# The first batch's step-1 sums in SBUF, turned by PE, in a fused FFT-mix and SoLU kernel

## The chip, the cores and the metric

The kernel runs on one core of one Trainium2 chip. The metric is the device time of one launch in microseconds, from the start of the program to its end. Engines are called as the profile calls them: PE (TensorE matmul), PEld (its weight load), DVE (VectorE), ACT (ScalarE), POOL (GpSimd), SP (SyncE, which here issues nearly all DMAs).

## What is computed

Eight batches of 3136 tokens with 256 channels. Along the tokens a real Fourier transform is taken, the spectrum is mixed by a complex 256x256 weight, biased and soft-thresholded, and transformed back; each token of the result then goes through a SoLU layer with 1024 hidden channels and a layer norm.

```python
X = rfft(x, axis=1); Xr, Xi = X.real, X.imag
Yr = Xr @ w_r - Xi @ w_i + b_r
Yi = Xr @ w_i + Xi @ w_r + b_i
Y  = soft(Yr, 0.01) + 1j * soft(Yi, 0.01)          # soft: sign(v) * max(|v| - 0.01, 0)
y  = irfft(Y, n=3136, axis=1)                       # 8 x 3136 x 256
h  = y @ w_in                                       # 25088 x 1024
s  = h * softmax(h)
out = (layernorm(s) * g_ln) @ w_out                 # 25088 x 256
```

## The kernel before

**The transform in two steps.** 3136 is 98 x 32. Step 1 sums over 98 (token index n1) for each of 32 n2; step 2 sums over the 32. The inverse has the same two steps. Step 1 of batches 0 and 1 is `fwd1_plain`: eight tiles of 98 x 1024 (n1 on the partitions, four n2 x 256 channels along them), in each two matmuls with the 98x98 matrix `fa_s` as the stationary operand and 512 columns of x moving, all in f32. ACT copies the sums out of PSUM, and SP stores them to a DRAM tile `s1f`. Step 2 needs pairs of (frequency, n2) on the partitions, so `load_bin` loads them back from `s1f` in that order: six groups `g` of four blocks of 128 x 256, and a last half block in `fwd2_last`. Each block is scaled by `scales[b]["s1"]`, a power of two found from the peak of x, and split into a high and a low f16 half (`bin`), the high half by ACT, the low by DVE. `fwd2` multiplies them with `fb_s`, `mix` with the complex weights, `threshold` follows, `inv1` is the first inverse step, whose sums are stored to DRAM (`s2f`, for batch 0), and `inv2` loads them back into `zt` tiles, makes the second inverse step with `iaf_s` and fills `ring_hi` and `ring_lo`, the tokens for SoLU. `moe_head`, `moe_turn` and `moe_tail` are SoLU for 128 tokens each.

**Weights.** The mix weights `w_hi`, `w_lo` have five parts; three are made early, and `later_mix_weights` makes the other two from sums and differences. Their raw matrices lie in two tiles named `zt` (lines 1169 to 1172), of a pool with two buffers of that name: the first loads of `inv2` reuse these buffers. `moe_w_in` loads and splits w_in into `win_hi`, `win_lo`, `win_low`; `moe_w_out` and `finish_w_out` do so with w_out. Their scales are found from a peak over all partitions, by a reduction on DVE, a transpose on PE (`ident,wpeak` in the profile), a reduction of the row (`wtop`), and a product with ones that spreads it.

**What sets the order.** All operations of the program are recorded first, and a planner (`Plan`, lines 286 to 495) then puts them in a fixed order on each engine; all instructions are issued on line 396. It is a list scheduler: an operation has a key (`nc.key`, a smaller key is more urgent), a length estimated in `weigh`, and the operations that it needs; on the engine that can start first, the one with the smallest key is taken among those that can start within 105 ns of the first. An operation gives no urgency to those that it needs. Tiles of one name get their buffers in turn, and a buffer is free again when the last operation that reads it is done. `nc.hold(op)` makes an operation wait for another one that it doesn't need. Each engine then works its own list strictly in order, so that a waiting instruction holds up all behind it, and a waiting DMA on SP all later DMAs of SP. The keys of the parts are in `KEYS` (lines 42 to 53): the first part of the program has keys from -200, `later_mix_weights` has 254.87, and the first `inv2` has -122.76.

**Lines touched.** `fwd1_plain` 709, `load_bin` 747, `fwd2_last` 775, `x_scale` 618, `w3` 1169, `win_*` 1239, `wout` 1241, `ring_lo` 1028, `moe_w_out` 1277, and the main part from 1344.

## Time and profile before

| | us |
|---|---|
| median of 3 runs (lowest, highest) | 1536.11 (1534.29, 1539.84) |
| span of the profiled execution | 1532.7 |
| PE busy in it | 1506.8 (98%) |
| DVE busy | 1223.0 (80%) |
| ACT busy | 1182.7 (77%) |
| POOL busy | 1139.1 (74%) |
| median minus span | 3.4 |

The profile is one execution on the chip, seen by the hardware profiler. An engine's busy time is the time in which it has an instruction in work; an idle time is put down to what released the next instruction. The granted clock is what PE was given in a stretch, 1.00 for 2.4 GHz and 0.50 for 1.2 GHz. An f32 matmul leaves two records in the trace, a transpose or an f16 matmul one. Line L396 stands on all rows, since all instructions are issued there; the tile names tell them apart, with buffer numbers left out (`w_hi` for w0_hi and w1_hi).

### The profile page before, as it was taken

The numbers are of one execution on the slowest core, as the hardware profiler recorded it, in microseconds if no ns is written. First come the engines' busy times: TensorE is split into PE (matmuls) and PEld (weight loads), VectorE is DVE, ScalarE is ACT, GpSimd is POOL, SyncE is SP. The second block draws the span as 40 slices with busy tenths as digits, with TensorE's granted clock in tenths as the row PEclk, the third lists the DMA queues.
The fourth block names the chain that finished last, engine by engine and source line by source line (L and its number), as shares of the span: only waits on it lengthen the run. The fifth ranks groups of instructions, "written<-read, shape, count | busy, mean of one in ns | idle before, by whom it ended". The sixth has DMA issues, their size and how long they took to land.

```text
span 1532.7 us, 40928 instructions
## 1 busy us (share of the span) xinstructions
PE 1506.8 (98%) x15375; PEld 1064.5 (69%) x15375; DVE 1223.0 (80%) x2496; ACT 1182.7 (77%) x2140; POOL 1139.1 (74%) x1652
## 2 busy tenths in 40 slices
PE   6989999999999999999999999999999999999998
PEld 3446777668766777677776777677776777776666
DVE  5888788888997988978788878978788778766664
ACT  5777878887797778877887778887788777777775
POOL 0656988777886887778876787758878688876776
PEclk8989999999999999999999999999999999999999
DMA  7777965999699987999689995899877976687666
GB/s 255 216 252 179 203 135 108 219 220 234 154 205 241 232 169 182 214 232 221 116 187 214 237 211 128 193 244 223 162 165 169 219 152 128 134 160 156 141 123 121
DMA packets 531580, 285.61 MB, mean 186 GB/s; under 512 B 426501, under 2 KB 504689, under 8 KB 531381
## 3 DMA queue, kind: packets, MB, share of 16 engines
q1 hardware_dynamic: 530932, 281.39, 83.0%
q8 instruction: 120, 1.97, 0.5%
q10 hardware_dynamic: 448, 1.61, 0.3%
q14 instruction: 80, 0.65, 0.1%
HBM read 103.07 MB, written 77.07 MB: 118 GB/s over the span
## 4 chain that ended last, share of the span: by engine, by line
PE 90%; DMA 3%; ACT 3%; POOL 2%; DVE 1%; issue 1%; SPq 0%; ACTq 0%; DVEq 0%; POOLq 0%
PE banks L396 90%; DMA xt<-in_x_dram 1%; DMA zt<-s2f 0%; DMA u<-in_x_dram 0%; POOL y L396 0%; DMA xt<-s1f 0%; POOL ll L396 0%; DMA zt<-in_w_r_dram 0%; ACT Xh L396 0%; DVE yt L396 0%; POOL r L396 0%; DMA zt<-s 0%; ACT zout L396 0%; DVE Xl L396 0%; SPq L396 0%
## 5 line engine op out<-in xcount | busy, mean ns | idle before, releaser
L396 POOL TENSOR_TENSOR ll<-u,lh 128x1024 f16<-128x1024 f32 x196 | 425.4, 2171 | 110.7 <-ACT lh L396 105.5
L396 PE MATMUL banks<-wout,th 128*128 128x256 f16 x3136 | 374.5, 273 | 0.2 <-DVE zout L396 0.2
L396 PEld LDWEIGHTS <-th 128*128 128x128 f16 x3136 | 304.5, 98 | 61.0 <-issue 1.9
L396 DVE SCALAR_TENSOR_TENSOR u<-banks,sm,u 128x1024 f32<-128x1024 f32 x196 | 251.1, 1281 | 105.0 <-ACT u L396 80.4
L396 DVE TENSOR_REDUCE sm<-banks 128x1 f32<-128x1024 f32 x196 | 239.2, 1220 | 79.8 <-PE banks L396 78.9
L396 PE MATMUL banks<-win_hi,ring_hi 128*128 128x512 f16 x768 | 292.0, 380 | 0.0
L396 PE MATMUL banks<-win_lo,ring_hi 128*128 128x512 f16 x768 | 291.8, 380 | 0.0
L396 PE MATMUL banks<-win_low,ring_lo 128*128 128x512 f16 x768 | 291.7, 380 | 0.0
L396 ACT CAST lh<-u 128x1024 f16<-128x1024 f32 x196 | 205.4, 1048 | 111.5 <-POOL a L396 57.2
L396 ACT ACTIVATE u<-banks,sm,hsb 128x1024 f32<-128x1024 f32 x192 | 231.2, 1204 | 61.3 <-DVE sm L396 51.6
L396 PEld LDWEIGHTS <-ring_hi 128*128 128x128 f16 x1536 | 148.7, 98 | 141.8 <-issue 2.3
L396 ACT ACTIVATE junk<-u,sm 128x1024 bf16<-128x1024 f32 x196 | 226.0, 1153 | 3.2 <-DVE u L396 3.1
L396 PE MATMUL banks<-wout,tl 128*128 128x256 f16 x1568 | 203.4, 273 | 0.0
L396 POOL TENSOR_TENSOR y<-yt,yc 128x512 f32<-128x512 f32 (+1 forms) x104 | 142.1, 1370 | 48.1 <-DVE yc L396 33.3
L396 PEld LDWEIGHTS <-tl 128*128 128x128 f16 x1568 | 151.8, 98 | 23.9 <-issue 1.0
L396 PE MATMUL banks<-w_hi,Xh 128*128 128x256 f16 (+1 forms) x584 | 165.4, 283 | 2.2 <-ACT Xh L396 1.8
L396 PE MATMUL banks<-w_hi,Xl 128*128 128x256 f16 (+1 forms) x584 | 165.0, 283 | 1.5 <-POOL Xl L396 0.9
L396 PE MATMUL banks<-w_lo,Xh 128*128 128x256 f16 (+1 forms) x584 | 165.2, 283 | 0.0
L396 POOL TENSOR_SCALAR a<-a,hsb 128x1 f32<-128x1 f32 x384 | 128.3, 334 | 14.7
L396 PEld LDWEIGHTS <-ring_lo 128*128 128x128 f16 x768 | 75.2, 98 | 91.1 <-issue 0.6
L396 PEld LDWEIGHTS <-Xh 128*128 128x128 f16 x1168 | 112.9, 98 | 31.7 <-issue 5.2
L396 POOL TENSOR_TENSOR yl<-y,yh 128x512 f16<-128x512 f32 x96 | 116.9, 1220 | 16.6 <-ACT yh L396 15.8
(177 smaller groups left out, 2512.6 us busy)
## 6 DMA issues: line engine op xcount, KB each, us to landing
xt<-in_x_dram SPq DMA_DIRECT2D x104, 392.0 KB
zt<-s SPq DMA_DIRECT2D x56, 392.0 KB
s<-zout SPq DMA_DIRECT2D x42, 512.0 KB
s<-av SPq DMA_DIRECT2D x48, 392.0 KB
bin<-s SPq DMA_DIRECT2D x36, 512.0 KB
out_dram<-o SPq DMA_DIRECT2D x128, 96.0 KB
out_dram<-o SPq DMA_DIRECT2D x136, 64.0 KB
out_dram<-o SPq DMA_DIRECT2D x128, 32.0 KB
```

The lines of the kernel that those rows point to most:

```text
L396: getattr(engine, name)(*args, **kw)
```

## The change

For batch 0 `fwd1_first` takes the place of `fwd1_plain`: the operands change sides, so that 128 channels of x for one n2 are the stationary operand and the 98 columns of `fa_s` move. The sums come out with channels on the partitions, and ACT writes them, permuted, into a constant tile `home` (seen as f32 through `at`). Nothing of batch 0 is stored to `s1f` or loaded from it. `turn_bin` transposes blocks of 128x128 from `home` into PSUM on PE, four in one bank, held until the scale is known (`scaled[0]`), and ACT and DVE scale and split them directly from there, in 12 halves where 6 wholes were before. Later `home` is used again: `win_hi`, `win_lo`, `win_low`, `wout` and `ring_lo` are now parts of it. Loads that were held on the loads from `s1f` are held on step 1 (`done[0, c]`) or on the transposes (`turned[g]`), and the keys of the scale become -170 and -165.

```diff
@@ -356,7 +357,7 @@
-            n = moving.cells.size * (4 if moving.dtype == F32 else 1) * 0.42 + 1
+            n = moving.cells.size * (2 if name == "transpose" else 4 if moving.dtype == F32 else 1) * 0.42 + 1
@@ -596,12 +597,15 @@
+    home = const.tile([P, 2 * ND * N1 * N2], F16, name="home")
+    at = home.bitcast(F32).rearrange("p (h c n) -> p h c n", h=ND, c=N1)
...
-    peaks, scales = {}, {}
+    peaks, scales, scaled = {}, {}, {}
@@ -632,7 +636,7 @@
-        nc.vector.tensor_scalar(sc[:, 4:], sc[:, :1], S_SCALE, None, ALU.mult)
+        scaled[0] = nc.vector.tensor_scalar(sc[:, 4:], sc[:, :1], S_SCALE, None, ALU.mult)
@@ -706,43 +710,75 @@
     PLAIN, PLAIN_Z = 2, 1
     done = {}
+    def fwd1_first(c):
+        n2 = C1 // D
+        pool, name = (mp, "u") if c % 2 == 0 else (xp, "xt")
+        xt = pool.tile([P, C1], F32, name=name, bufs=4)[:N1]
+        queue = nc.scalar if c % 2 else nc.sync
+        queue.dma_start(xt, x[0].rearrange("(n1 n2) d -> n1 (n2 d)", n1=N1)[:, c * C1 : (c + 1) * C1])
+        note_peak(0, c, N2 // n2, xt)
+        for dh in range(ND):
+            pa = front_psum(0)
+            with nc.together():
+                for i in range(n2):
+                    nc.tensor.matmul(pa[:, i * N1 : (i + 1) * N1], xt[:, i * D + dh * P : i * D + (dh + 1) * P], fa_s, start=True, stop=True)
+            to = at[:, dh, :, c * n2 : (c + 1) * n2].rearrange("p c n -> p n c")
+            done[0, c] = nc.scalar.copy(to, pa[:, : n2 * N1].rearrange("p (n c) -> p n c", c=N1))
     def fwd1_plain(b, c):
         if c == 0:
             s1[b] = dram.tile([N1, N2, D], F32, name="s1f")
         n2 = C1 // D
-        pool, name, bufs = (mp, "u", 4) if b == 0 and c % 2 == 0 else (xp, "xt", 4)
-        xt = pool.tile([P, C1], F32, name=name, bufs=bufs)[:N1]
-        if b and c < 4:
-            nc.hold(raw[0, 4])
-        queue = nc.scalar if b == 0 and c % 2 else nc.sync
-        queue.dma_start(xt, x[b].rearrange("(n1 n2) d -> n1 (n2 d)", n1=N1)[:, c * C1 : (c + 1) * C1])
+        xt = xp.tile([P, C1], F32, name="xt", bufs=4)[:N1]
+        if c < 4:
+            nc.hold(done[0, NCH - 1])
+        nc.sync.dma_start(xt, x[b].rearrange("(n1 n2) d -> n1 (n2 d)", n1=N1)[:, c * C1 : (c + 1) * C1])
         note_peak(b, c, N2 // n2, xt)
-        whole = b or c < 6
-        if whole:
-            pool, name, bufs = (xp, "av", 2) if b else ((fp, "zout", 3), (fp, "bin", 3), (xp, "av", 2))[c % 3]
-            av = pool.tile([P, C1], F32, name=name, bufs=bufs)[:N1]
-            parts = [(av, 0, n2)]
-        else:
-            parts = [(mp.tile([P, HF], F32, name=name, bufs=3)[:N1], i * n2 // 2, n2 // 2) for i, name in enumerate(("th", "tl"))]
+        av = xp.tile([P, C1], F32, name="av", bufs=2)[:N1]
         for h in range(C1 // HF):
             hs = slice(h * HF, (h + 1) * HF)
-            to = parts[0][0][:, hs] if whole else parts[h][0]
             pa = front_psum(b)
-            nc.reserve(to)
+            nc.reserve(av[:, hs])
             nc.tensor.matmul(pa[:N1], fa_s, xt[:, hs], start=True, stop=True)
-            done[b, c] = nc.scalar.copy(to, pa[:N1])
-        for av, i, n in parts:
-            nc.sync.dma_start(s1[b][:, c * n2 + i : c * n2 + i + n], av.rearrange("p (n d) -> p n d", d=D))
+            nc.scalar.copy(av[:, hs], pa[:N1])
+        nc.sync.dma_start(s1[b][:, c * n2 : (c + 1) * n2], av.rearrange("p (n d) -> p n d", d=D))
     QG = 4
-    raw = {}
+    turned = {}
     s2 = {}
     zouts = {}
     Xs, Ys = {}, {}
+    def turn_bin(g):
+        load_after(fb_s[g], fb[:, g * QG : (g + 1) * QG], done[0, 4] if g == 0 else done[0, NCH - 1])
+        load_after(gb_s[g].rearrange("p u r t m -> p u (r t) m"), gb[:, g * QG // 2 : (g + 1) * QG // 2].rearrange("p u r t m -> p u (r t) m"), done[0, NCH - 1])
+        if g == 0:
+            for to, src in ((gs_s, gs), (fs_s, fs), (iaf_s, iaf), (fa16_s, fa16), (ia_s, ia)):
+                load_after(to, src, done[0, NCH - 1])
+        parts = fp.tile([P, QG, 2, D], F16, name="bin", bufs=3)
+        k = scales[0]["s1"]
+        flat = at.rearrange("p h c n -> p h (c n)")
+        for j in range(QG // 2):
+            pt = front_psum(0)
+            qs = slice(2 * j, 2 * j + 2)
+            nc.reserve(parts[:, qs])
+            nc.hold(scaled[0])
+            with nc.together():
+                for i in range(2):
+                    for dh in range(ND):
+                        q = g * QG + 2 * j + i
+                        to = pt[:, (i * ND + dh) * P : (i * ND + dh + 1) * P]
+                        turned[g] = nc.tensor.transpose(to, flat[:, dh, q * P : (q + 1) * P], ident)
+            pv = pt.rearrange("p (q d) -> p q d", d=D)
+            nc.scalar.activation(parts[:, qs, 0], pv, AF.Copy, scale=k)
+            nc.vector.scalar_tensor_tensor(parts[:, qs, 1], pv, k, parts[:, qs, 0], ALU.mult, ALU.subtract)
+        return parts
     def load_bin(b, g):
@@ -751,18 +787,11 @@
+        if b == 0:
+            return turn_bin(g)
...
-        if b:
-            t = fp.tile([P, QG, D], F32, name="bin", bufs=3)
...
-            t = xp.tile([P, C1], F32, name="xt", bufs=4).rearrange("p (q d) -> p q d", d=D)
-        raw[b, g] = nc.sync.dma_start(t, v[:, g * QG : (g + 1) * QG])
...
-        if b == 0:
-            load_after(fb_s[g], fb[:, g * QG : (g + 1) * QG], raw[0, g - 1] if g else done[0, NCH - 1])
-            load_after(gb_s[g].rearrange("p u r t m -> p u (r t) m"), gb[:, g * QG // 2 : (g + 1) * QG // 2].rearrange("p u r t m -> p u (r t) m"), raw[b, g])
+        t = fp.tile([P, QG, D], F32, name="bin", bufs=3)
+        nc.sync.dma_start(t, v[:, g * QG : (g + 1) * QG])
@@ -781,9 +810,18 @@
             for t in range(2):
                 nc.sync.dma_start(bt[t * half : (t + 1) * half], s1[b][4 * Q :, :, t].rearrange("c n d -> (c n) d"))
         else:
-            raw_s = fp.tile([P, D], F32, name="bin_s", bufs=1)
-            for t in range(2):
-                nc.sync.dma_start(raw_s[t * half : (t + 1) * half], s1[b][4 * Q :].rearrange("c n d -> (c n) d"))
+            if b:
+                raw_s = fp.tile([P, D], F32, name="bin_s", bufs=1)
+                for t in range(2):
+                    nc.sync.dma_start(raw_s[t * half : (t + 1) * half], s1[b][4 * Q :].rearrange("c n d -> (c n) d"))
+            else:
+                raw_s = front_psum(0)[:, :D]
+                both = fp.tile([P, 2, D], F32, name="yt")[:, 0].rearrange("p (h t m) -> p h t m", h=ND, t=2)
+                for t in range(2):
+                    nc.vector.tensor_copy(both[:, :, t].rearrange("p h (c n) -> p h c n", n=N2), at[:, :, 4 * Q :])
+                with nc.together():
+                    for dh in range(ND):
+                        nc.tensor.transpose(raw_s[:, dh * P : (dh + 1) * P], both[:, dh].rearrange("p t m -> p (t m)"), ident)
             bt = fp.tile([P, D], F16, name="bin_s16", bufs=1)
             k = scales[b]["s1"]
             nc.scalar.activation(bt, raw_s, AF.Copy, scale=k)
@@ -1025,7 +1063,8 @@
-    ring_lo = const.tile([P, ND, R], F16, name="ring_lo")
+    at_ring = 3 * ND * FF + 2 * FF // P * D
+    ring_lo = home[:, at_ring : at_ring + ND * R].rearrange("p (e r) -> p e r", e=ND)
@@ -1160,7 +1199,7 @@
-        fwd1_plain(0, c)
+        fwd1_first(c)
@@ -1169,7 +1208,7 @@
-            load_after(w3[h][:, j], w[h * P : (h + 1) * P], done[0, 3])
+            load_after(w3[h][:, j], w[h * P : (h + 1) * P], done[0, 1])
@@ -1236,9 +1275,10 @@
-    win_hi, win_lo, win_low = (const.tile([P, ND, FF], F16, name=f"win_{v}") for v in ("hi", "lo", "low"))
+    win_hi, win_lo, win_low = (home[:, i * ND * FF : (i + 1) * ND * FF].rearrange("p (e f) -> p e f", e=ND) for i in range(3))
...
-    wout = const.tile([P, NF, 2, D], F16, name="wout")
+    at_wout = 3 * ND * FF
+    wout = home[:, at_wout : at_wout + 2 * NF * D].rearrange("p (f j e) -> p f j e", f=NF, j=2)
@@ -1278,14 +1318,14 @@
-        nc.hold(raw[0, 3])
+        nc.hold(turned[3])
...
-            load_wide(wo_s[f // 2], w_out[f * P : (f + 2) * P].rearrange("(f p) e -> p f e", p=P), raw[0, 3])
+            load_wide(wo_s[f // 2], w_out[f * P : (f + 2) * P].rearrange("(f p) e -> p f e", p=P), turned[3])
@@ -1341,15 +1381,15 @@
-    nc.key = -150
+    nc.key = -170
...
-    nc.key = -140
+    nc.key = -165
...
-    moe_w_in(0, raw[0, 0])
+    moe_w_in(0, done[0, NCH - 1])
...
-    moe_w_in(1, raw[0, 1])
+    moe_w_in(1, turned[1])
```

How the change moves instructions stands at three places.

PE at the end of batch 0's step 1, up to the first step-2 matmul of `fwd2` (`top` is the row of peaks of x, `v,ones` and `u,ones` spread the scales and sum the mix weights, `fb` is the step-2 matrix). Before:

```order
L396 MATMUL banks<-u,fa_s 98x512 x2
L396 MATMUL banks<-xt,fa_s 98x512 x2
L396 MATMUL banks<-ident,top 1x98
L396 MATMUL banks<-v,ones 128x1
L396 MATMUL banks<-u,ones 128x256 x4
L396 MATMUL banks<-v,ones 128x1
L396 LDWEIGHTS bin
L396 MATMUL banks<-fb_221,bin 128x2x32
```

After:

```order
L397 MATMUL banks<-fa_s,u 128x98 x8
L397 MATMUL banks<-u,ones 128x256 x4
L397 MATMUL banks<-fa_s,u 128x98 x16
L397 MATMUL banks<-ident,top 1x98
L397 MATMUL banks<-v,ones 128x1
L397 MATMUL banks<-ident,home 128x128 x20
L397 MATMUL banks<-v,ones 128x1
L397 MATMUL banks<-ident,home 128x128 x4
L397 LDWEIGHTS bin
L397 MATMUL banks<-fb_286,bin 128x2x32
```

The transposes (`ident,home`) stand on both sides of the second spreading of scales and ahead of the first `fb` matmul; 24 of the 48 come before it.

DVE around the last products that read the weights' raw tiles (`w_lo<-zt`, of `later_mix_weights`). Before, where they stand ahead of the first halves of `bin`:

```order
L396 TENSOR_SCALAR bias_y<-bias_t,sc 128x512
L396 TENSOR_SCALAR un<-un,w_un 128x1
L396 SCALAR_TENSOR_TENSOR w_lo<-zt,w_sc,w_hi 128x256 x4
L396 SCALAR_TENSOR_TENSOR bin<-xt,sc,bin 128x4x256
L396 SCALAR_TENSOR_TENSOR bin_s_294<-bin_s,sc,bin_s_294 64x256
L396 SCALAR_TENSOR_TENSOR bin<-xt,sc,bin 128x4x256
```

After, where `unscale` and `scale` belong to w_out, `yt` to the mix of batch 1 and `hsb` to its scales:

```order
L397 TENSOR_SCALAR scale<-scale 128x1
L397 TENSOR_SCALAR unscale<-unscale 128x1
L397 SCALAR_TENSOR_TENSOR w_lo<-zt,w_sc,w_hi 128x256 x2
L397 SCALAR_TENSOR_TENSOR yt<-banks,un,bias_y 128x512 x2
L397 TENSOR_SCALAR un<-banks 128x2
L397 TENSOR_SCALAR hsb<-un,win_un 128x1
```

The last two of the four have moved from about the fortieth to about the two hundredth instruction of DVE's list, behind the preparation of w_in and w_out and the first units of batch 1's step 2.

SP around the first loads of the second inverse step, `zt<-s2f`. Before:

```order
L396 DMA s2f<-zout 128x2x256 x2
L396 DMA s2f<-zs 64x256
L396 DMA u<-in_moe_w_out_dram 128x2x512
L396 DMA s1f<-av 98x1024
L396 DMA u<-in_moe_w_out_dram 128x2x512
L396 DMA zt<-s2f 98x1024 x2
L396 DMA s1f<-av 98x1024 x2
L396 DMA xt<-in_x_dram 128x784
```

After:

```order
L397 DMA bin_s<-s1f 64x256 x2
L397 DMA bin<-s1f 128x4x256
L397 DMA xt<-in_x_dram 128x784
L397 DMA xt<-in_x_dram 98x1024 x2
L397 DMA bin<-s1f 128x4x256
L397 DMA xt<-in_x_dram 98x1024 x2
L397 DMA bin<-s1f 128x4x256
L397 DMA s_1823<-zs 64x512
L397 DMA zt<-s2f 98x1024 x2
L397 DMA bin<-s1f 128x4x256
```

The loads of `zt` have moved behind loads of batch 1's step 2 (`bin<-s1f`) and of later x (`xt<-in_x_dram`), and behind the store of batch 1's first inverse sums (`s_1823<-zs`).

## Rows read from the trace of the kernel before

**Rows 1.** The page: span, and busy time, share and instructions of TensorE.
```profile
span 1532.7 us, 40928 instructions
...
PE 1506.8 (98%) x15375; PEld 1064.5 (69%) x15375; DVE 1223.0 (80%) x2496; ACT 1182.7 (77%) x2140; POOL 1139.1 (74%) x1652
```

**Rows 2.** Busy time by stretch: us; PE, PEld, DVE, ACT, POOL; clock, DMA share, GB/s.
```profile
0.00:44.16 44.16, 31.44 (x184) 16.53 (x184) 25.32 (x62) 22.91 (x43) 3.50 (x10) 0.85 0.79 252
44.16:93.00 48.84, 47.89 (x607) 22.88 (x602) 41.35 (x61) 39.72 (x78) 37.52 (x27) 1.00 0.71 212
93.00:121.64 28.64, 22.28 (x112) 12.18 (x111) 22.68 (x61) 16.75 (x37) 9.50 (x8) 0.70 0.79 253
...
200.00:1532.00 1332.00, 1327.78 (x13815) 957.28 (x13813) 1066.97 (x2168) 1038.16 (x1866) 1020.78 (x1506) 1.00 0.85 182
```

**Rows 3.** PE timeline, 20 to 45 us: start, duration, instruction, idle ahead and releaser.
```profile
20.54 1.88 PE L396 MATMUL banks<-xt,fa_s 98*98 98x512 f32 x4
...
23.64 1.99 PE L396 MATMUL banks<-u,ones 128*128 128x256 f32 x8
...
33.23 0.29 PE L396 MATMUL banks<-fb,bin 64*128 64x64 f16 x4 [5.67 <-ACT bin L396]
...
37.69 0.61 PE L396 MATMUL banks<-w_hi,Xh 128*128 128x512 f16 x1 [1.79 <-ACT Xh L396]
...
42.20 0.63 PE L396 MATMUL banks<-w_hi,Xh 128*128 128x512 f16 x1
42.63 0.58 PE L396 MATMUL banks<-w_lo,Xh 128*128 128x512 f16 x1
...
43.35 0.87 PE L396 MATMUL banks<-fb,bin 64*128 64x64 f16 x48
44.16 0.39 PE L396 MATMUL banks<-w_hi,Xh 128*128 128x512 f16 x1
```

**Rows 4.** Pieces of the chain that ended last, before 125 us: start, duration, what.
```profile
29.29 6.21 DMA xt<-s1f
...
103.43 7.23 DMA zt<-s2f
```

**Rows 5.** DVE timeline, 24 to 35 us.
```profile
24.13 0.15 DVE L396 TENSOR_SCALAR sc<-sc 128x1 f32<-128x1 f32 x1
...
30.00 1.78 DVE L396 SCALAR_TENSOR_TENSOR w_lo<-zt,w_sc,w_hi 128x256 f16<-128x256 f32 x4
33.21 1.28 DVE L396 SCALAR_TENSOR_TENSOR bin<-xt,sc,bin 128x1024 f16<-128x1024 f32 x1 [1.43 <-ACT bin L396]
```

**Rows 6.** PE timeline, 89 to 132 us.
```profile
89.51 0.27 PE L396 MATMUL banks<-w_hi,Xh 128*128 128x256 f16 x1
89.62 0.27 PE L396 MATMUL banks<-w_lo,Xh 128*128 128x256 f16 x1
...
93.40 0.27 PE L396 MATMUL banks<-ident,wpeak 128*1 128x128 f32 x1
...
110.80 6.68 PE L396 MATMUL banks<-iaf_s,zt 98*128 98x98 f32 x32 [3.46 <-DMA zt<-s2f]
...
131.66 1.93 PE L396 MATMUL banks<-iaf_s,zt 98*128 98x98 f32 x16
```

**Rows 7.** ACT's groups, 0 to 30 us: busy us, mean ns, idle ahead.
```profile
L396 ACT COPY av<-banks 98x512 f32<-98x512 f32 x4 | 2.3, 585 | 1.6 <-PE banks L396 1.6
```

**Rows 8.** DVE's groups, 19 to 130 us.
```profile
L396 DVE TENSOR_SCALAR junk<-u 128x512 uint32<-128x512 uint32 x8 | 3.3, 415 | 0.0
...
L396 DVE SCALAR_TENSOR_TENSOR win_lo<-u,win_sc,win_hi 128x1024 f16<-128x1024 f32 x2 | 2.5, 1266 | 0.0
...
L396 DVE TENSOR_REDUCE peaks<-xt 128x1 f32<-128x784 f32 x2 | 1.9, 952 | 0.0
...
L396 DVE TENSOR_REDUCE mx<-th 128x1 f32<-128x512 f32 x2 | 1.4, 676 | 0.0
...
L396 DVE TENSOR_SCALAR hsb<-hsb 128x1 f32<-128x1 f32 x6 | 0.9, 145 | 0.0
```

More of the change, by code (lines that the diff above doesn't have):

```diff
@@ L156, in bitcast @@
     def bitcast(self, dtype):
-        return self._then(self.cells, "bitcast", dtype, dtype=dtype)
+        n = mybir.dt.size(dtype) // mybir.dt.size(self.dtype)
+        return self._then(self.cells[..., ::n] if n > 1 else self.cells, "bitcast", dtype, dtype=dtype)
     def unsqueeze(self, i):
@@ L753, in load_bin @@
             return t
+        if b == 0:
+            return turn_bin(g)
         v = s1[b][: 4 * Q].rearrange("(q c) n d -> q (c n) d", c=4).rearrange("q r d -> r q d")
-        if b:
-            t = fp.tile([P, QG, D], F32, name="bin", bufs=3)
-        else:
-            t = xp.tile([P, C1], F32, name="xt", bufs=4).rearrange("p (q d) -> p q d", d=D)
-        raw[b, g] = nc.sync.dma_start(t, v[:, g * QG : (g + 1) * QG])
-        if b == 0 and g == 0:
-            for to, src in ((gs_s, gs), (fs_s, fs), (iaf_s, iaf), (fa16_s, fa16), (ia_s, ia)):
-                load_after(to, src, raw[0, 0])
-        if b == 0:
-            load_after(fb_s[g], fb[:, g * QG : (g + 1) * QG], raw[0, g - 1] if g else done[0, NCH - 1])
-            load_after(gb_s[g].rearrange("p u r t m -> p u (r t) m"), gb[:, g * QG // 2 : (g + 1) * QG // 2].rearrange("p u r t m -> p u (r t) m"), raw[b, g])
+        t = fp.tile([P, QG, D], F32, name="bin", bufs=3)
+        nc.sync.dma_start(t, v[:, g * QG : (g + 1) * QG])
         parts = fp.tile([P, QG, 2, D], F16, name="bin", bufs=3)
```

## The prediction, made before the changed kernel ran

> **What bounds the kernel now.** The page comes first: TensorE (PE) is busy 1506.8 of 1532.7 us [rows 1]. Then the table by stretch [rows 2]: from 200 us on PE works 1327.78 of 1332.00 us, so a change to the start can only move the time through PE work added or taken away, PE idle time, and PE time at the lower of its two clock levels (1.2 instead of 2.4 GHz) in the first 122 us. There the reader should see two holes: 0 to 44.16 us with a granted clock of 0.85 and 31.44 us busy, and 93 to 121.64 us with 0.70 and 22.28 us; between them PE is busy 47.89 of 48.84 us at 1.00.
>
> The PE timeline says what the first hole is [rows 3]: batch 0's step 1 ends at about 22.3 us, the first step-2 matmul starts at 33.23 after 5.67 us of waiting for `bin`, and the twelve mix matmuls from 37.69 on run 0.43 us apart (42.20 to 42.63) until the clock is back at 43. The sums go out and come back meanwhile: the load that the chain goes through is issued at 29.29 and takes 6.21 us of it [rows 4]. The scale that step 2 needs is ready at 24.28 [rows 5]. So the change takes away the round trip, some 9 us between scale and first use.
>
> The second hole stands behind `wpeak` at 93.40 [rows 6]: the inverse of batch 0 (`iaf_s,zt`) starts at 110.80 after 3.46 us of waiting for the load of `zt`, whose load is 7.23 us of the chain [rows 4], and runs at the low clock: 32 records in 6.68 us, while 16 take 1.93 at 131.66 (0.12 each).
>
> **The change part by part.**
> Step 1. Before, a 98x512 matmul is two records and takes about 0.86 us (two of them 1.88 with the drain of the last [rows 3]): 16 make 13.8. After, the 98x98 f32 form of `iaf_s,zt` does it, two records of 0.123 each [rows 6]: 64 x 0.246 = 15.7. **+2.0 us**, on the path while x arrives early enough; ends near 25.1 instead of 22.3, with the other small work of the start.
>
> Transposes. 50 of 128x128 f32. The only 128x128 one of the trace, `ident,wpeak`, has one column and lasts 0.27 alone [rows 6]; in a row the form of `iaf_s,zt`, 0.12 a record at the high clock and 0.21 at the low, is nearest in shape. I take 0.123: **+6.2 us** (10.5 at the low clock, 13.5 at 0.27). A page of the Trainium skill, TensorE: Matmul & The Clock Gate (Part 4: PE-mode transpose), puts a transpose in a kernel at about 275 ns; by it they would be 13.75 us, and no row here shows them in a row.
>
> Copies on ACT. 16 copies of 98x512 become 16 of 128x4x98 into `home`, elements 128 B apart. The row is 0.585 each for a contiguous copy [rows 7]: 9.4 us in 17 us of PE work, hidden; no row prices the stride. I take no penalty; at three times (28 us) the copies end near 35 us and hold the transposes, +6. The Trainium skill, SBUF — State Buffer (Door 1: The DMA port swizzle), says that accesses pay when each falls in another 16-byte line; by that the copies would be the dearer case, and no run shows it yet.
>
> The scale. It does not come at once: DVE now has five 512-column operations in front of it (0.4 to 0.7 each [rows 8]), and step 1 ends 2.8 later, so I put it at 29.2 instead of 24.3. Then four transposes, one ACT piece, step 2: `fb` at about 33, and the first mix 4.5 us behind it as before (33.23 to 37.69): 38 (36.5 to 41). The round trip is gone, but the first mix starts no earlier; what is won is that 24 transposes and the tail of step 1 lie in the hole, and that PE is likely to have the high clock again (12 mix at 0.22 instead of 0.43, 2.6 us).
>
> From first mix to `wpeak`. Before: 12 mix (2.6), `fb` (0.8, from 43.35 to 44.16), the stretch of 48.84, and 0.4 up to `wpeak` = 52.6 at the high clock. The order takes out of it one unit's 12 wide and 12 narrow mix (3.9), one unit's inverse step (0.8) and two step-1 matmuls (1.7) with trifles (0.2), and puts in 16 transposes (2.0): 52.6 - 6.6 + 2.0 = 48. `wpeak` at **86** (84.5 to 89).
>
> The load of `zt`: here something new appears. The two `zt` buffers hold the mix weights at first. The last reader before was `w_lo` at 30.00 [rows 5], in the stretch in which DVE waited for `bin` (idle 1.43 at 33.21). That hole is closed, so the planner puts these `w_lo` at their low priority: two of them behind everything that DVE does for w_in, for w_out and for batch 1's first units. The reload of `zt` on SyncE's queue waits for them, behind it stand all later loads, and PE waits in `iaf_s,zt`. In DVE's order, from the reduction of `wpeak` to these two, stand 104 instructions: 8 reductions of 784 columns at 0.95 = 7.6; 4 of 1024 columns at 1.27, 5.1; 14 reductions and scaled sums of 512 at 0.68, 9.6; 14 single-operand ones of 512 at 0.42, 5.9; 15 of 256 at 0.445 (four in 1.78 [rows 5]), 6.7; 3 single-operand ones of 256, by half the wide ones' price at least, 0.9; 46 small ones at about 0.16, 7.5 (all prices without a group: [rows 8]). Sum 43.3. Records of neighbours overlap a little, so 40 to 43; I take 41.5. For waits I add 3: DVE is busy 22.68 of 28.64 us in the second hole, which at that share would be 10.7, but PE has more to give it now; 0 and 10 are the ends. The load is 6.2 to 7.2 [rows 4]; I take 6.2.
> So `iaf_s,zt` starts at 86 + 41.5 + 3 + 6.2 = **136.7** instead of 110.80.
>
> Work drawn forward. Ahead of `iaf_s,zt` PE now also does 96 `fb` (2 x 0.81 = 1.6), 36 narrow mix (0.11 each [rows 6], 4.0), 8 products with `ones` (four take 1.99 [rows 3]; 3.7) and small pieces (1.2): 10.5 us that it need not do later. The transposes and step 1 are already inside 136.7. Behind it the clock comes back as before (low from 110.80 to about 121 there), so that cancels.
> **Sum:** 136.7 - 110.8 - 10.5 = **+15.4**. On the profiled execution: 1532.7 + 15.4 = 1548.1; the median of the runs lies 3.4 above that span (1536.11), so **1551.5 us**. Its own range: 84.5 + 40 + 0 + 6.2 = 130.7 gives +9.4; 144 gives +22.7; 1545.5 to 1559.
>
> The loads and stores that go (8 tiles stored, 6 and a part loaded) leave queue time free and cost nothing on the path after 44 us; the loads of `fb` and `gb` start earlier. That `home` also holds win and wout makes their first writes wait for the last transposes, which end long before `wpeak`: nothing. The 24 halves of `bin` in place of 12 whole cost ACT and DVE 6 more starts each, some 1 us in a stretch where DVE is busy 41.35 of 48.84: nothing on the path.
>
> **The rivals.**
> *Faster: PE's own work covers the reload.* Between `wpeak` and `iaf_s,zt` PE now has 10.5 drawn forward + 6.6 taken behind `wpeak` + 6.4 that was there before = 23.4 us. If the tile came free in time, `iaf_s,zt` would start at 86 + 23.4 + 2 = 111.4: 111.4 - 110.8 - 10.5 = -9.9, **1526**. For it: the reload waits in the trace for its data only. Against: DVE would have to pass 104 instructions in 19 us. It decides where `iaf_s,zt` starts before 113.6.
> *About the same.* The first mix comes at 34 instead of 38 (the scale early, the transposes at once), and DVE meets no wait: 82 + 40 + 0.3 + 4.2, with a load a third shorter than the rows, 126.5: +5.2, **1541**. It needs all three, or that part of the DVE list runs before `wpeak`, which its order excludes.
> *Copies bind (stride).* +6 on top: **1557**. For it: nothing in the trace; a stride of 128 B isn't in it. It would show in the duration of the copies.
> *Transposes at 0.27.* 13.5 instead of 6.2 us, **1559**. For it: the one row of a transpose; against: that one stands alone and its end is modelled.
> *The change doesn't do what it says* (the wait for `bin` stays as long because another input is late) goes with the second and third: the first mix would then be at 41 and the sum +18.
>
> **How the numbers follow.** Forecast 0.57; copies 0.10; transposes 0.08; about the same 0.19; faster 0.06. Within 0.5%, about what a measurement of this kernel can tell from no change, is 1528.4 to 1543.8. Faster 0.06, same 0.19, slower 0.75. The range takes in the rivals above and most of the one below, 1537 to 1562; left out are the faster case and the upper end of DVE's waits with a dear copy.
>
> **What would show each step.** In the profile after: 98x98 records 0.12 apart from 6 to 25 us; transposes 0.12 apart from 29 us; `wpeak` near 86; DVE busy with little pause from there to 130; the last `w_lo` reading `zt` near 130, the issue of `zt<-s2f` right behind it, and a PE wait of over 10 us in all between 90 and 137, with the clock low in it. If the first wait is gone but `zt<-s2f` is issued before 110, the step on the tile is wrong and the time is below 1530. If the copies last over 1 us each, or the first mix starts after 41, the part on step 1 is wrong, and the time is higher by as much.

## The result, and the profile after

The changed kernel takes 1551.21 us (median of 4 runs, 1549.81 to 1555.06) against 1536.66 for the kernel before (4 runs, 1534.29 to 1539.84): ratio 1.0097, 95% interval 1.0077 to 1.0117. It is slower, by about 14.6 us. The profiled execution has a span of 1550.3 us, 17.6 more than that of before [rows 1].

The page of after: span; busy us, share and instructions of each engine.

```profile
span 1550.3 us, 41192 instructions
...
PE 1522.8 (98%) x15521; PEld 1090.8 (70%) x15521; DVE 1224.7 (79%) x2504; ACT 1187.5 (77%) x2146; POOL 1136.6 (73%) x1652
```

Where the 17.6 us lie is read from two tables by stretch, cut at `wpeak` (93.40 before, 91.34 after) and at 140 us. Columns as in [rows 2]. The kernel before:

```profile
0.00:93.40 93.40, 79.72 (x785) 39.46 (x785) 66.67 (x121) 63.03 (x122) 41.42 (x37) 0.93 0.75 231
93.40:140.00 46.60, 40.20 (x262) 24.32 (x260) 39.57 (x112) 30.20 (x62) 20.20 (x22) 0.82 0.79 247
140.00:1532.70 1392.70, 1386.85 (x14332) 1000.72 (x14330) 1116.79 (x2264) 1089.51 (x1958) 1077.47 (x1595) 1.00 0.85 181
```

The kernel after:

```profile
0.00:91.30 91.30, 87.18 (x852) 58.89 (x853) 62.58 (x121) 61.56 (x113) 33.29 (x34) 0.89 0.57 168
91.30:140.00 48.70, 30.44 (x308) 19.28 (x306) 41.19 (x112) 28.73 (x57) 18.53 (x18) 0.75 0.81 240
140.00:1550.30 1410.30, 1405.16 (x14363) 1012.64 (x14363) 1120.90 (x2273) 1097.24 (x1979) 1084.82 (x1602) 1.00 0.83 179
```

Stretch less busy time is PE's idle time: 13.7, 6.4 and 5.9 us before; 4.1, 18.3 and 5.1 after. So the change does what it says: the first hole lost 9.6 us. The second gained 11.9, the rest lost 0.7: +1.6 us of idle time in all. The other 16.0 us are busy time: about 8 of it is added work (2.0 for step 1, 50 transposes at 0.12). The rest goes with a lower clock: by an estimate from the profiles (PE's busy time times the share of the clock that it lacked, in stretches of 5 us up to 200 us) that took 11.2 us before and 21.3 after. The two come to 18 us for the 16.0 measured, so they are rough.

Most of that lower clock stands in a place where the kernel before had none. First before, then after, in stretches of 5 us:

```profile
15.00:20.00 5.00, 5.00 (x13) 1.94 (x12) 2.20 (x3) 3.36 (x7) 0.00 (x0) 1.00 0.90 292
```

```profile
15.00:20.00 5.00, 5.00 (x25) 5.00 (x25) 3.89 (x4) 2.51 (x3) 1.73 (x3) 0.50 0.92 244
20.00:25.00 5.00, 5.00 (x18) 3.98 (x18) 0.15 (x1) 2.49 (x8) 0.00 (x0) 0.50 0.08 23
25.00:30.00 5.00, 5.00 (x18) 4.28 (x17) 0.00 (x0) 1.51 (x2) 0.00 (x0) 0.50 0.44 118
30.00:35.00 5.00, 3.93 (x33) 3.69 (x32) 2.37 (x12) 3.70 (x6) 0.00 (x0) 0.95 0.96 311
```

From 15 to 30 us PE is shown busy without a pause and has 0.50 (1.2 GHz). From 20 to 30 us DVE does next to nothing (0.15 and 0.00 us) and the DMA share is 0.08 and 0.44: what comes next waits for step 1. The PE timeline of after says in which instructions (start, duration, instruction, idle ahead and releaser):

```profile
17.23 3.62 PE L397 MATMUL banks<-fa_s,u 98*128 98x98 f32 x16
...
26.30 3.67 PE L397 MATMUL banks<-u,ones 128*128 128x256 f32 x8
29.76 4.08 PE L397 MATMUL banks<-fa_s,u 98*128 98x98 f32 x32
33.68 0.25 PE L397 MATMUL banks<-ident,top 98*1 98x98 f32 x1
...
35.72 2.40 PE L397 MATMUL banks<-ident,home 128*128 128x128 f32 x20
...
40.53 1.29 PE L397 MATMUL banks<-fb,bin 64*128 64x64 f16 x48
...
45.61 0.38 PE L397 MATMUL banks<-w_hi,Xh 128*128 128x512 f16 x1
```

The new form of step 1 runs at 0.226 us a record at 17.23 (3.62 / 16) and at 0.1275 at 29.76 (4.08 / 32), right behind eight records with 256 columns. Step 1 ends at 33.8 us, 11 later than before [rows 3]; `fb` starts at 40.53 without a wait for a load, but later than the 33.23 of before.

The second hole, on PE from `wpeak` to the inverse step [rows 6]:

```profile
91.34 0.27 PE L397 MATMUL banks<-ident,wpeak 128*1 128x128 f32 x1
...
114.32 0.58 PE L397 MATMUL banks<-v,ones 1*128 1x2 f32 x2 [7.76 <-DVE v L397]
120.25 0.61 PE L397 MATMUL banks<-fs_s,bin_s 128*128 128x128 f16 x4 [5.34 <-DVE bin_s L397]
...
139.91 7.12 PE L397 MATMUL banks<-iaf_s,zt 98*128 98x98 f32 x32 [0.35 <-DMA zt<-s2f]
```

The long waits are not for the load of `zt` (0.35) but for `v` and `bin_s`: the scale of batch 1 and the last group of its step-1 sums. Both stand late in DVE's list, as its timeline shows (start, duration, instruction; DVE has no pause ahead of the first two):

```profile
114.12 0.15 DVE L397 TENSOR_SCALAR v<-v 1x2 uint32<-1x2 uint32 x1
...
119.70 0.48 DVE L397 SCALAR_TENSOR_TENSOR bin_s<-bin_s,sc,bin_s 64x256 f16<-64x256 f32 x1
...
135.24 0.87 DVE L397 SCALAR_TENSOR_TENSOR w_lo<-zt,w_sc,w_hi 128x256 f16<-128x256 f32 x2
```

Besides, batch 1's sums still go through DRAM: the last store and the load of `bin_s` in SP's queue, and the load of `zt` behind the last `w_lo`:

```profile
109.56 0.53 SPq L397 DMA_DIRECT2D s1f<-av  x1
...
113.01 1.12 SPq L397 DMA_DIRECT2D bin_s<-s1f  x2
...
134.02 0.47 SPq L397 DMA_DIRECT2D s<-zs  x1
135.79 0.94 SPq L397 DMA_DIRECT2D zt<-s2f  x2
```

### The profile page after: what moved, and what is told of

It reads as the page before. It is cut to its first block, busy times and chain, and to the rows that moved or that the text cites. A ratio compares the mean times of both kernels' runs of the same rounds, so it can differ in the third digit from the quotient of the medians.

```text
span 1550.3 us, 41192 instructions
## 1 busy us (share of the span) xinstructions
PE 1522.8 (98%) x15521; PEld 1090.8 (70%) x15521; DVE 1224.7 (79%) x2504; ACT 1187.5 (77%) x2146; POOL 1136.6 (73%) x1652
## 4 chain that ended last, share of the span: by engine, by line
PE 94%; DVE 3%; DMA 2%; issue 0%; ACT 0%; ACTq 0%; SPq 0%; DVEq 0%
PE banks L397 94%; DMA xt<-in_x_dram 1%; DVE peaks L397 1%; DVE u L397 0%; DVE lh L397 0%; DMA fb<-in_fb_dram 0%; DMA zt<-s2f 0%; DMA gb<-in_gb_dram 0%; DVE Xl L397 0%; DVE sm L397 0%; DVE home L397 0%; DVE yt L397 0%; DVE bin L397 0%; DVE ll L397 0%; DVE w_lo L397 0%
## 5 line engine op out<-in xcount | busy, mean ns | idle before, releaser
L397 PE MATMUL banks<-home,ring_hi 128*128 128x512 f16 x1536 | 458.3, 380 | 0.7 <-DVE u L397 0.7
L397 PE MATMUL banks<-home,th 128*128 128x256 f16 x3136 | 374.5, 273 | 0.1
L397 PE MATMUL banks<-home 128*128 128x512 f16 x768 | 291.5, 380 | 0.0
L397 PE MATMUL banks<-home,tl 128*128 128x256 f16 x1568 | 203.3, 273 | 0.0
L397 PEld LDWEIGHTS <-home 128*128 128x128 f16 x768 | 75.3, 98 | 91.1 <-issue 0.6
L397 POOL TENSOR_TENSOR r<-r,mhalf 128x1 f32<-128x1 f32 x196 | 114.9, 586 | 10.9
```

The lines of the kernel that those rows point to most:

```text
L397: getattr(engine, name)(*args, **kw)
```

## Experiments

Each was timed against the kernel before, on the same chip. The changed kernel ("after") stands at the ratio 1.0097. In the code, `...` marks lines left out.

**The raw weights released early.** The prediction's theory is A: `iaf_s,zt` is late because the last `w_lo` keep the `zt` buffers. B is its rival. Two kernels make these products early. The first gives them an urgent key and lets the planner do the rest:

```diff
-    mix_w=254.87,
+    mix_w=-163.0,
```

> The key of later_mix_weights goes from 254.87 to -163, so that the zt tiles are free early and the planner lays the order anew: iaf_s,zt now stands ahead of batch 1's 96 fb and 36 narrow mix matmuls. Theory A (the second hole is made by the late release of the zt tiles, through the order that the planner builds around it): iaf_s,zt starts at 115 to 124 instead of 139.9, the batch-1 work fills PE behind it, 1538 to 1543 us. Theory B (VectorE's own load between wpeak and 135 us is the bound whatever the order): PE waits for VectorE somewhere else for as long, 1547 to 1552 us.

Measured: 1551.05 us, ratio 1.0096 (1.0079 to 1.0114). On PE:

```profile
118.64 3.71 PE L397 MATMUL banks<-iaf_s,zt 98*128 98x98 f32 x32
```

`iaf_s,zt` starts at 118.64 instead of 139.91, as A has it, and the time is the same, as B has it. The new plan changes more than this place: PE's idle time from 90 to 140 us falls from 18.3 to 14.2, and from 200 us on it rises from 5.1 to 9.9. The second kernel moves only these operations, behind the second group's `bin`, and leaves the rest of the order as in after:

```diff
+        moved = [op for op in order if op.key == KEYS["mix_w"]]
+        order = [op for op in order if op.key != KEYS["mix_w"]]
+        at = order.index(self.early) + 1
+        order[at:at] = sorted(moved, key=lambda op: op.seq)
```

> Only the operations of later_mix_weights move, to behind the second pair of bin halves; every other instruction keeps its place on its engine. Theory A' (the wait for the zt tile as such): the load of zt is issued more than 8 us earlier and the time falls to 1543 or less. Theory B' (in this order PE does batch 1's work ahead of iaf_s,zt, which keeps it till 139.5 anyway; the trace shows 0.35 us of waiting for zt): iaf_s,zt moves by less than 2.5 us, the time is 1548.5 to 1551.5.

Measured: 1549.11, ratio 1.0086 (1.0071 to 1.0101). DVE's, SP's and PE's timelines of this kernel:

```profile
45.13 1.68 DVE L404 SCALAR_TENSOR_TENSOR w_lo<-zt,w_sc,w_hi 128x256 f16<-128x256 f32 x4 [0.83 <-ACT w_hi L404]
```

```profile
133.98 0.47 SPq L404 DMA_DIRECT2D s<-zs  x1
134.50 1.00 SPq L404 DMA_DIRECT2D zt<-s2f  x2
```

```profile
114.40 0.58 PE L404 MATMUL banks<-v,ones 1*128 1x2 f32 x2 [7.76 <-DVE v L404]
120.33 0.61 PE L404 MATMUL banks<-fs_s,bin_s 128*128 128x128 f16 x4 [5.34 <-DVE bin_s L404]
...
140.52 3.78 PE L404 MATMUL banks<-iaf_s,zt 98*128 98x98 f32 x32 [0.99 <-DVE Xs L404]
```

The products are done by 47 us, and nothing follows from it: the load still stands behind `s<-zs` in SP's order, `iaf_s,zt` still behind batch 1's work in PE's, and the waits for `v` and `bin_s` are the same to 0.01 us. So A falls as a cause of the time. What the late tile can do, it does in planning: with the early key the planner puts `iaf_s,zt` ahead of batch 1's step 2, with the late one behind it, and on the chip PE then follows that order. But the first of the two kernels shows that the other order isn't faster by itself.

The traces show one more difference: a second stretch at the low clock, behind the second hole. First after, then the second kernel:

```profile
140.00:150.00 10.00, 10.00 (x40) 8.03 (x41) 5.08 (x18) 7.93 (x22) 6.83 (x9) 0.50 0.44 134
```

```profile
140.00:150.00 10.00, 9.48 (x66) 6.89 (x67) 8.02 (x22) 6.67 (x17) 8.41 (x10) 1.00 0.45 136
```

The 32 records of `iaf_s,zt` take 7.12 us in after and 3.78 here. That is some 5 us of PE time in these two executions; the medians differ by 2.1 us, and the intervals overlap. What sets the clock there was not tested.

A third kernel also put `iaf_s,zt` ahead of all of batch 1's later work in the list of after, without a new plan. Its operations no longer give the function's values, so its 1563.30 us (ratio 1.0175; 1543 or less was expected if the late load costs the time by itself, 1546 to 1551 if DVE's list does) decides nothing. Its trace has `iaf_s,zt` at 112.23 behind 8.11 us of waiting for `zt`, then waits of 11.01 for `v` and 6.10 for `bin_s`.

**The clock in step 1.** Two kernels keep the order and add PE work to step 1, of forms that the kernel has elsewhere at the high clock: six matmuls in the old form (98x512), or 28 f16 matmuls of 256 columns. The lines left out keep the planner from counting the added work, so that its order stays. The first:

```diff
+                if dh == 0 and c >= 2:
...
+                    nc.tensor.matmul(pa[:N1], fa_s, xt[:, :HF], start=True, stop=True)
...
```

> Six matmuls of the old step-1 form (98x512 moving, 0.86 us each at the high clock) are put between the 98-column matmuls of batch 0's step 1, one ahead of each tile from the third on; their result is overwritten; all else keeps its place. Theory C (the clock fell in step 1 because of the 98-column form): granted clock near 1.00 from 10 to 30 us, step 1 ends at 29 to 32 us instead of 33.8 though 5.2 us are added, time 1546 to 1550. Rival (the clock falls there whatever PE does): step 1 ends at 40 to 44, time 1557 to 1562.

Measured: 1544.61, ratio 1.0060 (1.0045 to 1.0075). The second:

```diff
+                if c >= 1:
...
+                    w16 = ones.bitcast(F16)
+                    for _ in range(2):
+                        nc.tensor.matmul(pa[:, :2 * P], w16[:, :P], w16, start=True, stop=True)
...
```

> 28 f16 matmuls of 256 columns (some 0.11 us each at the high clock) go between the 98-column matmuls, two ahead of each half tile from the second tile on; their result is overwritten; all else keeps its place. Theory C, if this much dense work is enough: clock near 1.00, step 1 ends at 28 to 30 us, time 1545 to 1549. Rival (the clock falls whatever PE does, or this is too little): step 1 ends at 37 to 41, time 1554 to 1559.

Measured: 1543.07, ratio 1.0047 (1.0027 to 1.0067). The stretches and the PE timeline of this second kernel:

```profile
15.00:20.00 5.00, 5.00 (x41) 4.48 (x40) 3.10 (x3) 4.52 (x9) 0.23 (x1) 1.00 0.75 192
20.00:25.00 5.00, 5.00 (x40) 4.66 (x40) 1.38 (x8) 2.72 (x4) 0.00 (x0) 1.00 0.48 134
```

```profile
16.01 1.95 PE L401 MATMUL banks<-fa_s,u 98*128 98x98 f32 x16
...
27.24 0.25 PE L401 MATMUL banks<-ident,top 98*1 98x98 f32 x1
...
38.02 0.38 PE L401 MATMUL banks<-w_hi,Xh 128*128 128x512 f16 x1
```

With about 3 us of extra work step 1 ends 6.4 us earlier (`top` at 27.24 for 33.68), at 1.00 throughout, and the first mix comes at 38.02, where the prediction had it (38). The time falls by 0.0050 of 1536, some 8 us (some 6 with the old form), a little below what theory C expected of each kernel and far below its rival. These are net gains: the added matmuls are PE work of some 3 and 5 us themselves. So the clock in step 1 was one price of the change, and with PE busy in both cases it went with the kind of matmul. The low clock isn't gone from the kernel: behind `top` PE idles, and from 29.27 to 33.30 us it has 0.58 and takes 4.05 us for twenty transposes.

**DVE's list shortened before the inverse.** All of batch 2's early work (peaks and scale) is moved from ahead of `iaf_s,zt` to right behind its first half:

```diff
...
+        moved = [op for op in order[:at] if op.tag == "front2"]
+        order = [op for op in order[:at] if op.tag != "front2"] + [order[at]] + moved + order[at + 1 :]
```

> Everything of batch 2 (the loads of x for its peak, eight reductions of 0.95 us on VectorE, its scale) that stood ahead of iaf_s,zt goes behind it; the rest keeps its place. Theory B (VectorE's load between 92 and 135 us is what PE waits for): VectorE's list there is 9 us shorter, iaf_s,zt starts at 130 to 134, time 1541 to 1546. Rival (the round trip of batch 1's step-1 sums through DRAM, last store at 109.6, bin_s ready at 119.7, holds PE anyway): PE waits for bin_s in place of v, iaf_s,zt at 136 or later, time 1548 to 1552.

Measured: 1561.08, ratio 1.0162 (1.0143 to 1.0181). The PE timeline:

```profile
134.66 3.70 PE L406 MATMUL banks<-iaf_s,zt 98*128 98x98 f32 x16 [0.94 <-DMA zt<-s2f]
149.65 0.37 PE L406 MATMUL banks<-ident,top 128*1 128x128 f32 x1 [11.29 <-DVE top L406]
```

`iaf_s,zt` does start 5.3 us earlier, but the moved block came in one piece and PE now waits 11.29 us for its `top`. The time lies above both expected ranges. As a test of what the list is worth this is inconclusive: the new place made a new wait.

**One instruction of the list.** The last DVE instruction that forms `v` (0.15 us) is moved to where its operands are ready:

```diff
+        op = self.marks["v"]
+        order.remove(op)
+        at = 1 + max(order.index(o) for o in op.needs)
+        order.insert(at, op)
```

> On the changed kernel, one VectorE instruction of 0.15 us moves: the last one of batch 1's scale (v, 1x2), from behind 19 others (114.1 us) to right behind its own input (103.6). PE waited 7.8 us for it. If that wait is a cost by itself: v,ones at about 104 instead of 114.3, time 1541 to 1545. If the next wait is behind it anyway (bin_s, whose data come back from DRAM after the last store at 109.6): PE waits 13 us for bin_s in place of 7.8 and 5.3, iaf_s,zt within 1 us of 139.9, time 1549 to 1552.

Measured: 1549.03, ratio 1.0080 (1.0064 to 1.0096). The timelines of PE, ACT and DVE:

```profile
105.82 0.38 PE L407 MATMUL banks<-v,ones 1*128 1x2 f32 x2
120.50 0.61 PE L407 MATMUL banks<-fs_s,bin_s 128*128 128x128 f16 x4 [14.30 <-DVE bin_s L407]
```

```profile
117.98 0.51 ACT L407 ACTIVATE bin_s<-bin_s,sc 128x256 f16<-128x256 f32 x1 [3.89 <-DVE sc L407]
```

```profile
119.96 0.48 DVE L407 SCALAR_TENSOR_TENSOR bin_s<-bin_s,sc,bin_s 64x256 f16<-64x256 f32 x1
```

The 7.76 us for `v` went whole into the wait for `bin_s`, which stayed at 120: a covered wait. What ends last at `bin_s` is DVE's list: from 102 us on DVE shows no wait, and it comes to its half of `bin_s` 1.5 us after ACT is done with the other half (118.49). The load, issued at 112.6, is in by 117.98 at the latest. How much earlier it came isn't shown; if it came just then, a shorter list alone gains at most some 2 us there.

**What the transposes cost.** Each of the 48 is issued twice, in the order of after:

```diff
...
+                        nc.tensor.transpose(to, flat[:, dh, q * P : (q + 1) * P], ident)
...
                         turned[g] = nc.tensor.transpose(to, flat[:, dh, q * P : (q + 1) * P], ident)
```

> On the changed kernel, each of the 48 transposes of turn_bin is done twice into the same place; all else keeps its place. If the added PE work of the change counts in full (as the sum of the forecast took it, 0.12 us each): 5.2 to 6.5 us more than the changed kernel, 1555 to 1558. If part of it lies under waits that are there anyway (the second hole, where PE waits for data from DRAM): 0 to 4 us more, 1550 to 1554. If a transpose costs 0.27 us: 13 us more.

Measured: 1552.08, ratio 1.0111 (1.0096 to 1.0126). The PE timeline:

```profile
35.34 4.58 PE L401 MATMUL banks<-ident,home 128*128 128x128 f32 x40
...
115.88 0.58 PE L401 MATMUL banks<-v,ones 1*128 1x2 f32 x2 [6.47 <-DVE v L401]
```

Forty take 4.58 us, 0.115 each, so the added work is some 5.5 us. `wpeak` moves from 91.34 to 93.02, and the wait for `v` gets shorter by 1.3 of these 1.7 us. So waits that are there anyway hide a part of it. How much of it reaches the time isn't shown: the ratios differ by 0.0014, less than their intervals, and from 140 to 150 us PE has 1.00 here where after has 0.50.

**Both repaired.** Here the planner is told what the new form takes (246 ns a matmul in place of the 166 that its formula gives), the weights are made early by their key, and step 1 has the f16 filler; the order is planned anew:

```diff
-    mix_w=254.87,
+    mix_w=-163.0,
...
+            if moving.dtype == F32 and moving.cells.size == N1 and name != "transpose":
+                n = 246.0
...
```

> The planner is told that a 98-column f32 matmul takes 246 ns instead of 166, later_mix_weights gets the early key of e1, and the f16 filler of e4 holds the clock in step 1; the planner then lays the order anew, with token matmuls between batch 1's units behind iaf_s,zt. Theory (both holes are made by two separate things, the low clock in step 1 and an order in which VectorE is late): the low clock is gone and the second hole smaller, 1530 to 1538 us. Rival (VectorE's load is the bound in any order): 1540 to 1547, as e4.

Measured: 1539.84 (10 runs), ratio 1.0023 (1.0014 to 1.0033), the best of all, still not below before; it lies between the two expected ranges. Without the early key (`mix_w` as in after), with the filler and this alone:

```diff
+            if moving.dtype == F32 and moving.cells.size == N1 and name != "transpose":
+                n = 246.0
...
```

> e9 without the early key of the later mix weights: the planner is told 246 ns for a 98-column f32 matmul and the f16 filler holds the clock in step 1. If e9's gain over e4 came from the place of iaf_s,zt (111.3 there, ahead of batch 1's step 2): here iaf_s,zt stands behind batch 1's first units again and the time is that of e4, 1541 to 1546. If it came from the better costs alone: 1537 to 1541.

Measured: 1545.33, ratio 1.0067 (1.0051 to 1.0084). The inverse step starts at 124.00 there and at 111.31 with the key; 5.5 us of the medians go with that (6.8 by the ratios), where the same key gave nothing without the filler and the planner's new price. It isn't the second hole that got smaller: PE's idle time from 90 to 140 us is 13.7 us with the key and 13.8 without. With the key it starts as early as in the kernel before, but still behind waits:

```profile
106.88 0.55 PE L403 MATMUL banks<-v,ones 1*128 1x2 f32 x2 [6.76 <-DVE v L403]
111.31 7.12 PE L403 MATMUL banks<-iaf_s,zt 98*128 98x98 f32 x32 [3.88 <-DMA zt<-s2f]
```

Two more kernels start from the one with both repairs and try to close this hole. In the first, batch 1's scale is more urgent (the rest of its edit is that of the kernel with both repairs):

```diff
-            nc.key = key
+            nc.key = -125.0 if fn is x_scale and b == 1 else key
```

> As e9, with the key of batch 1's scale at -125 instead of -1.5; the planner lays the order anew. Theory (what is left of the second hole is then the way of batch 0's inverse sums through DRAM, which the kernel before has too): the wait of 6.8 us for v goes and the wait for zt grows from 3.9 to 8 or more, time 1536 to 1540. Rival (the wait for v was a cost by itself): 1531 to 1535.

In the second, on top of that, w_out's preparation is less urgent (a smaller key is more urgent):

```diff
-    w_out=(-63.87, -1.11),
+    w_out=(-4.0, -1.11),
```

> As e11, and w_out's preparation gets key -4 instead of -63.87, so that VectorE does it behind batch 1's first units. If VectorE's list around 92 to 125 us is what makes PE idle there: 1529 to 1535. If PE's idle time there is the wait for data from DRAM, and w_out is missed later by the first tokens: 1538 to 1546.

Measured: 1548.01, ratio 1.0073 (1.0056 to 1.0090), and 1551.34, ratio 1.0093 (1.0078 to 1.0108). Both expectations of the time were missed. PE in the first of the two at the inverse step, then from 200 us to the end in it and in the kernel with both repairs:

```profile
111.52 7.12 PE L403 MATMUL banks<-iaf_s,zt 98*128 98x98 f32 x32 [11.14 <-DMA zt<-s2f]
```

```profile
200.00:1545.40 1345.40, 1333.28 (x13842) 960.19 (x13840) 1075.57 (x2168) 1041.80 (x1875) 1024.14 (x1512) 1.00 0.84 180
```

```profile
200.00:1538.80 1338.80, 1331.89 (x13845) 960.36 (x13842) 1069.44 (x2172) 1041.31 (x1874) 1026.66 (x1512) 1.00 0.85 182
```

The wait for `v` is gone, and `iaf_s,zt` stands where it stood, with 11.14 us of waiting for its own load: again a covered wait. The price came elsewhere: 12.1 us idle from 200 us to the end, where the kernel with both repairs has 6.9 and the kernel before, also to its end, 4.9. In the second kernel 11.7 us stand between 140 and 200 us. The new order of the whole program moves the time by several us either way; its places were not traced one by one.

## Why the prediction came out as it did

The forecast of 1551.5 us meets 1551.21, and the mechanism is only half right. Step by step:

- **Step 1 (+2.0 us, end at 25.1)** is the term that was mis-sized: it ended at 33.8. The price of a record, 0.123, holds at the high clock (1.95 us for 16 in the kernel with the f16 filler), but from 15 to 30 us it was 0.226. The prediction priced all 128 records at 0.123 and did not ask what clock PE would have in a long row of them. A warning stood in [rows 6], where the same form takes 6.68 us for 32 records; the prediction noted the low clock there and still took the high one for step 1.
- **Transposes (0.123 each)** held: 20 in 2.40 us. The group's row of after, 35 to 41 us (busy us, mean ns of one; idle ahead), shows why the rival of 0.27 looked right:

```profile
L397 PE MATMUL banks<-ident,home 128*128 128x128 f32 x24 | 3.1, 277 | 0.3 <-DVE bin L397 0.3
```

  A record lasts 277 ns, but the next one starts 0.12 us behind it, so that 24 keep PE busy for 3.1 us. The Trainium skill, TensorE: Matmul & The Clock Gate (Part 4: PE-mode transpose), has about 275 ns for one in a kernel (there in bf16). The trace agrees as to one transpose's duration; in a row the distance counts, and that rival falls.
- **Copies on ACT (0.585, no penalty)** were too cheap, as ACT's groups of after, 0 to 100 us, show (busy us, mean ns; idle ahead and its releaser):

```profile
L397 ACT COPY home<-banks 128x392 f32<-128x392 f32 x16 | 13.4, 837 | 14.9 <-PE banks L397 14.7
```

  They take 0.837 for 392 columns where 512 contiguous ones took 0.585 [rows 7]: 1.9 times as long per element. The spread elements are the main difference; no run takes them by themselves. That is the direction of what the Trainium skill, SBUF — State Buffer (Door 1: The DMA port swizzle), says of accesses that each fall in another 16-byte line; it gives no size. But ACT waited 14.7 us for PE ahead of them, and the last copy ends at 35.06, ahead of the first transpose at 35.72: they don't bind, and that rival falls too.
- **Scale at 29.2, first mix at 38 (36.5 to 41)**: 37.3 and 45.61, late by what step 1 was late. The text had said that a first mix after 41 makes the part on step 1 wrong; it is.
- **First mix to `wpeak`, 48 us**: 45.7. `wpeak` at 91.34, outside of 84.5 to 89.
- **DVE's list of 104 instructions, 41.5 + 3 us**: 43.3, from the reduction of `wpeak` (92.79) to the end of the last `w_lo` (136.1). It held within 1.2 us, but as a sum: DVE was busy 37.8 of these 43.3 us and waited 5.5, for 41.5 and 3 forecast.
- **The load of `zt`, 6.2 us**: 3.8 from the end of the last `w_lo` to `iaf_s,zt`, which starts at 139.91 for 136.7 forecast. That PE would wait there is wrong: it waits 0.35 us for the load and 13 for `v` and `bin_s` ahead of it. The "wait of over 10 us in all between 90 and 137" came, for other operands than forecast.
- **The sum**: by the formula 139.91 - 110.80 - 10.5 = +18.6; the spans differ by 17.6, the medians by 14.6, where the forecast was +15.4. The first mix was 7.6 us late; a way to `wpeak` 2.3 shorter than forecast and a load 2.4 shorter gave most of that back, and the place of the inverse step in the order measures a delay whose cause lies in other waits. That the forecast lies within 0.3 us of the measured time is in good part luck of such cancelling. (Two small slips in the sums, 23.4 for 23.5 in the faster rival and 10.7 for 10.9 in DVE's waits, change nothing.)
- **The faster rival** (1526 if `iaf_s,zt` starts before 113.6): the kernel with both repairs starts it at 111.31 and takes 1539.84. That is no test of its price: there `iaf_s,zt` stands ahead of batch 1's step 2, so that the 10.5 us drawn forward, which the rival takes off, aren't ahead of it. What it shows is that once PE comes to it early, batch 1's scale and the load of `zt` itself are late next. In the changed kernel the rival's condition was not met.

What the runs show as the cause: of the 14.6 us, some 6 to 8 were the clock in step 1, net of the fillers' own work. The order that is planned moves several us more: 5.5 between the two plans with and without the early key, though that key gave nothing in the plan of after, and against the f16 filler in the order of after (1.0047) the best kernel gains 0.0024, with intervals that overlap. With both repaired some 3 us remain. In that kernel PE's idle time is 25.6 us (span 1538.8 less 1513.2 busy), as before the change (25.9), and its busy time is 6.4 us longer. That fits PE work that the change adds (step 1's new form and the transposes, in place of a way through DRAM on which PE waited) and the filler's some 3 us; no run takes these apart.

Open is what would close the second hole. PE's idle time from 90 to 140 us is 13 to 19 us in every kernel with the change that gives the function's values, where it was 6.4 before. DVE is busy in most of it, and in the order of after its list is what ends last, at `v` and at `bin_s`, with the load of `bin_s` close behind it (where only the mix weights' products were moved, ACT's half waits for that load until 118.38, and DVE comes to its half at 119.79). One DRAM round trip, batch 0's inverse sums or batch 1's step-1 sums, stands in it each time; no run took either away alone. Nor was a version found that beats the kernel before.

## What to carry to other kernels

A busy engine is not an engine at full clock: before a matmul's operands change sides, look in the trace for the new form over a long stretch and read its granted clock there. And a round trip taken away at the head of a list-scheduled program is worth only what the order behind it can use; ask which operand is late next on each engine, and price the work that moves onto the bounding engine in full.

## What was not expected of the hardware

- The granted clock fell to 0.50 with PE shown busy 5.00 of 5.00 us in three stretches running, mostly in f32 matmuls of 98 columns; it was back at 0.95 in the stretch 30 to 35 us, behind eight records of 256 columns. With 28 f16 matmuls of 256 columns strewn among the same work it was 1.00 from 15 to 25 us.
- Behind the second hole the same 32 records of 98 columns took 7.12 us at 0.50 in after and 3.78 and 3.79 at 1.00 in two kernels of nearly the same order, which start them at 140.52 and 140.12 instead of 139.91.
- Transposes of 128x128 f32 in a row take 0.115 to 0.12 us each at the high clock, and 0.20 in the kernel with the f16 filler, where the clock was 0.58 in their stretch.
- A copy of ACT from PSUM into elements 128 B apart took 0.837 us for 392 columns, one into contiguous ones 0.585 for 512.
